# The first partial sum of three of four feature groups formed by two transfers instead of a GpSimd addition, and the third sum moved one up-projection later

## The chip, the cores and the metric

One core of one Trainium2 chip. The metric is the device time of one execution in microseconds (us); smaller is better. Engines: PE is TensorE (PEld its weight load), DVE is VectorE, ACT is ScalarE, POOL is GpSimd, SP is SyncE, which issues transfers only. SPq and POOLq are the queues of instructions that those engines hand out.

## The reference, cut to what matters

Two stages follow each other. The first is a block-wise linear attention with decay: for 4 sequences, 8 heads, 768 positions and head size 64, each block adds a masked product within the block and a product with a running state. The second is a feed-forward pair on the resulting 3072 x 512 rows:

```python
h = x @ w_in                                              # 512 -> 2048
g = np.maximum(h, 0.0) + alpha * np.minimum(h, 0.0)
return (g @ w_out).astype(np.float32)                     # 2048 -> 512
```

## The kernel before

The rows are worked in six chunks c = 0 to 5 of 512 rows each: a chunk is 256 positions of two sequences. For each chunk the attention part leaves its result transposed in `XT[c]`; `up` (L540) then makes one tile of 128 features by four products over the 512 inputs, 128x512 each, and ACT (L553) and DVE (L560) turn it into the f16 tile `g`. Sixteen `up` calls make a chunk's 2048 features. The output product of chunk c runs in the time of chunk c+1, a step of it after each `up` step, so that TensorE alternates between the two. What runs when is written out by hand: the calls stand in program order, each engine's queue keeps that order, and a framework adds the semaphore waits. The order of the last three chunks is in the table `plan` and the loop at L1070 to L1092 (U is one `up`, D one step of the output product).

For chunks 3, 4 and 5 the output product isn't done by 16 plain steps. The product of `g` (split in 2 halves of features and 2 halves of rows) with `w_out` (split in 2 by 2) uses a scheme of Winograd and Strassen with 7 products of half-size blocks instead of 8. `CHAIN` (L640) gives their order: 1, 2, 6, 5, 7, 3, 4. `product` (L642) does eight 128x256 products for one of them and one half b of its rows. Its inputs are sums of blocks of `g`, made by `g_sum` (L627), a 128x512 f16 operation for each of four feature groups j (two feature tiles of each half):

- S1 = a21 + a22, into the tile `s1` (`sums[3]`, one tile for all chunks)
- S3 = a11 - a21, over a21
- S2 = S1 - a11, over a11
- S4 = a12 - S2, over a12

Here a11, a12 are the blocks of the even rows and a21, a22 those of the odd ones. Product 1 reads a11 and product 2 a12 as they are; product 6 reads S2, product 5 reads S1 itself, product 7 reads S3, product 3 reads S4 and product 4 reads a22. S2 overwrites a11, so it comes after product 1; S1 of the next chunk overwrites `s1`, so it comes after product 5 of this one. S3 overwrites a21, so it comes after S1 has read it.

S1 and S3 of group j are made by `sums13` (L721) on POOL, when 10, 12, 14 and 16 `up` calls of the chunk are done (groups 0 to 3); group 3 of the last chunk is made on DVE. S2 and S4 are made on DVE in the next chunk (`sums_at`, L1062), and for the last chunk in `down2_last` (L704): it does products 1 and 2 by halves, then S2 for each half, and ends with products 3 and 4.

SP's queue in this stretch holds the transposing transfers of L311, the last loads, and the stores of the output (L589 for chunks whose output product is plain, L669 and L671 after that); each waits for its own data and is issued in order. POOL's queue holds, besides S1 and S3, `decayed` (L355), `key_decayed` (L291) and the loads of v that it issues (L278).

Of the kernel before, what the change touches and what calls it, by code (L numbers as in the profile page):

```python
# [11 lines left out]
def kernel(  # L12
# [16 lines left out]
    nc = tc.nc  # L29
# [5 lines left out]
    ALU = mybir.AluOpType  # L35
# [124 lines left out]
    for half in range(2):  # L160
# [7 lines left out]
        out=drop, in0=rel_i, scalar1=0.0, scalar2=-1e30, op0=ALU.is_lt, op1=ALU.mult  # L168
# [115 lines left out]
    def engine(x):  # L284
        return nc.gpsimd if x == "G" else nc.vector
# [242 lines left out]
    G = {}  # L528
    O = {}

    def group_of(c, j):
        if (c, j) not in G:
            G[c, j] = g_pool.tile([128, 2, 2, 2, 2, L], fp16, tag=f"g{j}", name=f"g{j}")
        return G[c, j]
# [5 lines left out]
    def up(c, f, bi=None, bank="h"):  # L540
        h_ps = bank_of(bank, "h_ps")
        n = CH if bi is None else W
        for gi in range(NHP):
            x = XT[c][:, gi]
            nc.tensor.matmul(  # L545
                h_ps[:, 0:n] if bi is None else h_ps[:, 0:n].rearrange("p (e j) -> p e j", e=2),
                lhsT=w_in_sb[:, gi, ts(f, 128)],
                rhs=x.rearrange("p e b j -> p (e b j)") if bi is None else x[:, :, bi, :],
                start=(gi == 0),
                stop=(gi == NHP - 1),  # L550
            )
        m = m_pool.tile([128, CH], fp32, tag="m", name="m")
        nc.scalar.activation(m[:, 0:n], h_ps[:, 0:n], AF.Relu, scale=-1.0)  # L553
        g = g_of(c, f)
        if bi is None:
            g, mv, hv = g.rearrange("p e b j -> p (e b j)"), m, h_ps
        else:
            g = g[:, :, bi, :]
            mv, hv = (y[:, 0:n].rearrange("p (e j) -> p e j", e=2) for y in (m, h_ps))
        nc.vector.scalar_tensor_tensor(  # L560
            out=g, in0=mv, scalar=oma[:, f : f + 1], in1=hv, op0=ALU.mult, op1=ALU.add
        )
# [4 lines left out]
    def down(c, t, part, nparts, bank="op"):  # L567
        if part == 0:
            O[c, t] = bank_of(bank, "o_ps")
        o_ps = O[c, t]  # L570
        n = NF // nparts
        for f in range(part * n, part * n + n):
            nc.tensor.matmul(  # L573
                o_ps,
                lhsT=lhs(c, f, t),
                rhs=w_out_sb[:, f, :],
                start=(f == 0),
                stop=(f == NF - 1),
            )
        if part == nparts - 1:  # L580
            store(c, t, o_ps, 0, DM)
            del O[c, t]
# [23 lines left out]
    sums = []  # L606
# [8 lines left out]
    def weight_sum(i, part):  # L615

        p = ds(2 * part, 2)
        (b11, b12), (b21, b22) = [[y[:, p] for y in x] for x in halves]
        w = [sums[x][:, p] for x in range(3)]
        out, in0, in1 = [(w[0], b12, b11), (w[1], b22, w[0]), (w[2], b21, w[1]), (b12, b22, b12)][i]  # L620
        nc.vector.tensor_tensor(out=out, in0=in0, in1=in1, op=ALU.subtract)

    def part_of(c, j, half, e, b=None):
        x = group_of(c, j)[:, half, :, e]
        return x.rearrange("p i b j -> p i (b j)") if b is None else x[:, :, b]

    def g_sum(c, i, j, eng, b=None):  # L627

        a11, a12, a21, a22 = [part_of(c, j, half, e, b) for e in range(2) for half in range(2)]
        s1 = sums[3].rearrange("p f (b j) -> p f b j", b=2)[:, ds(2 * j, 2)]  # L630
        s1 = s1.rearrange("p i b j -> p i (b j)") if b is None else s1[:, :, b]
        out, in0, in1, op = {
            1: (s1, a21, a22, ALU.add),
            3: (a21, a11, a21, ALU.subtract),
            2: (a11, s1, a11, ALU.subtract),
            4: (a12, a12, a11, ALU.subtract),
        }[i]
        engine(eng).tensor_tensor(out=out, in0=in0, in1=in1, op=op)  # L638
# [54 lines left out]
    def down2(c, x):  # L693

        i, side = CHAIN[x // 2]
        b = x % 2
        if b == 0 and i in (1, 2, 5):
            O[c, side] = bank_of("op" if side == 0 else "tk", "o_ps")
        t = O[c, side]
        product(c, i, b, t, b == 0 and i in (1, 2, 5), i in (2, 3, 4) and b == 1, ds(256 * b, 256))  # L700
        if b == 1:
            evacuated(c, i, t)

    def down2_last(c):  # L704
# [3 lines left out]
        for i, side, b in order:  # L708
# [8 lines left out]
            if i == 2 and b == 1:  # L717
                for j in range(4):
                    g_sum(c, 4, j, "V")

    def sums13(c, j, eng="G"):  # L721
        g_sum(c, 1, j, eng)
        g_sum(c, 3, j, eng)
# [346 lines left out]
    for c, at in plan.items():  # L1070
        u = d = w = 0
        for x, what in enumerate(order[c]):
            if x in at:
                at[x]()
            if what == "U":
                up(c, u // 2 + 8 * (u % 2), None, "h")
                u += 1
                if u in (10, 12, 14, 16):
                    sums13(c, u // 2 - 5, "V" if c == 5 and u == 16 else "G")
            elif c == 3:  # L1080
                down(c - 1, d // 4, d % 4, 4, ("op", "tk")[d // 4 % 2])
                d += 1
                for _ in range({1: 1, 3: 1, 4: 1, 7: 1, 8: 1, 10: 1, 11: 2, 12: 1, 14: 1, 15: 2}.get(d, 0)):
                    weight_sum(*divmod(w, 4))
                    w += 1
            else:
                down2(c - 1, d)
                d += 1
            if x in sums_at.get(c, {}):
                g_sum(c - 1, *sums_at[c][x])  # L1090
            if c == 4 and 10 <= x <= 13:
                weight_sum(3, x - 10)  # L1092
# [31 lines left out]
```

## Time and profile before

| what | value |
|---|---|
| runs | median 207.89 us (207.72 to 208.01, 3 runs) |
| profiled execution | 207.7 us, span 205.9 us |
| mean granted TensorE clock | 0.997 |
| DMA over the span | 31.16 MB, mean 151 GB/s |
| DMA in the stretch from 140 to 200 us | 27 to 66 GB/s in steps of 10 us |

The profile records one execution: for each engine its instructions with start, length and, where it stood idle before one, what ended the idle time. A row of the order of time reads: start, length, engine, line, operation, output<-inputs, sizes, and in brackets the idle time and its releaser; several instructions of one kind that follow each other are merged into a row with their count and the whole time they took. Ends of products on TensorE are modelled (they are pipelined), so the distance of their starts is what counts. A row of the view by stretches gives, after the stretch, its length, then busy time and count for PE, PEld, DVE, ACT and POOL, the granted clock, the DMA share and GB/s. A row of the waits gives the total, the number of times and the longest. A row of the transfers gives count, KB each and the median time from issue to landing.

### The profile page before, as it was taken

To read this page: it belongs to the slowest core of one execution; us is meant where nothing else is said; L and a number is where in the kernel's file an instruction comes from. 1 tells how busy PE (TensorE), PEld (TensorE's weight loads), DVE (VectorE), ACT (ScalarE), POOL (GpSimd) and SP (SyncE) were. 2 spreads that over 40 slices of the span, in tenths; PEclk is the share of its full clock that TensorE was granted. 3 is DMA by queue.
4 is the path that set the end of the run, shared out by engine and by line. 5 is a ranking of instruction groups with operands and counts; after the bars stand their busy time and mean duration, and the time that the engine had idled before them with its cause. 6 is when DMAs were issued, how large, how long until landed. Compare 5 with 4: busy or idle time off the path is not lost.

```text
span 205.9 us, 5567 instructions
## 1 busy us (share of the span) xinstructions
PE 200.3 (97%) x2263; PEld 122.8 (60%) x2263; DVE 159.5 (77%) x287; ACT 113.5 (55%) x210; POOL 110.0 (53%) x132
## 2 busy tenths in 40 slices
PE   7999999999999999999999999999999999999993
PEld 6976445556445465555555455467666666666882
DVE  6988889568889847899998897869999467675930
ACT  7896778144777118656766466463453544444321
POOL 8999794043487873295536994193094040553000
PEclk9999999999999999999999999999999999999998
DMA  5999999998999994999879973243001111011222
GB/s 159 280 196 233 244 261 207 233 284 241 224 279 282 198 261 111 232 159 143 170 109 276 212 180 82 42 106 45 30 0 54 51 54 51 2 51 54 75 79 102
DMA packets 58061, 31.16 MB, mean 151 GB/s; under 512 B 27108, under 2 KB 55796, under 8 KB 58036
## 3 DMA queue, kind: packets, MB, share of 16 engines
q1 hardware_dynamic: 42884, 21.25, 41.8%
q0 software_dynamic: 15136, 9.57, 29.2%
q8 instruction: 17, 0.28, 0.5%
q14 instruction: 8, 0.07, 0.1%
q10 hardware_dynamic: 16, 0.00, 0.0%
HBM read 27.27 MB, written 6.29 MB: 163 GB/s over the span
## 4 chain that ended last, share of the span: by engine, by line
PE 89%; ACT 4%; DVE 3%; issue 2%; ACTq 0%; DVEq 0%
PE h_ps L545 39%; PE o_ps L573 21%; PE o_ps L655 16%; PE s L391 3%; PE unread L152 3%; PE acc L416 2%; PE acc L375 2%; PE tpx L341 2%; DVE g L638 1%; PE acc L436 1%; DVE g L560 1%; ACT xT L250 1%; ACT L180 1%; ACT qkT L250 1%; ACT m L553 1%
## 5 line engine op out<-in xcount | busy, mean ns | idle before, releaser
L545 PE MATMUL h_ps<-xT,w_in_sb 128*128 128x512 f16 (+1 forms) x392 | 92.0, 375 | 0.4 <-DVE g L560 0.4
L560 DVE SCALAR_TENSOR_TENSOR g<-m,oma,h_ps 128x512 f16<-128x512 f32 (+1 forms) x98 | 70.9, 733 | 25.4 <-ACT m L553 22.4
L553 ACT ACTIVATE m<-h_ps 128x512 f32<-128x512 f32 (+1 forms) x98 | 57.3, 588 | 47.7 <-PE h_ps L545 40.5
L545 PEld LDWEIGHTS <-w_in_sb 128*128 128x128 f16 x392 | 37.6, 98 | 37.6 <-issue 0.6
L573 PE MATMUL o_ps<-w_out_sb,g 128*128 128x512 f16 x192 | 46.8, 380 | 0.0
L402 DVE TENSOR_TENSOR sm<-s,dmask 128x1024 f16<-128x1024 f32 x24 | 29.2, 1217 | 10.6 <-PE s L391 10.6
L655 PEld LDWEIGHTS <-g 128*128 128x128 f16 x288 | 27.9, 98 | 8.6 <-DVE g L638 0.4
L638 POOL TENSOR_TENSOR s<-g 128x512 f16<-128x512 f16 x11 | 13.0, 1184 | 34.9 <-DVE g L560 18.2
L573 PEld LDWEIGHTS <-g 128*128 128x128 f16 x192 | 17.7, 98 | 19.4 <-DVE g L560 0.2
L250 ACT ACTIVATE xT<-acc 128x512 f16<-128x512 f32 x24 | 14.3, 597 | 24.0 <-PE acc L436 22.2
L355 POOL TENSOR_TENSOR qdT<-qkT,qdecay 128x512 f16<-128x512 f16 (+1 forms) x19 | 20.9, 1102 | 7.3 <-DMA qkT<-qk 4.4
L655 PE MATMUL o_ps<-w_out_sb,g 128*128 128x256 f16 x192 | 24.2, 273 | 0.1
L291 POOL TENSOR_TENSOR kdec<-kraw,kdecay 128x512 f16<-128x512 f32 x18 | 19.1, 1064 | 5.5 <-DMA kraw<-in_k_dram 5.4
L254 POOL CAST qk<-qraw 128x512 f16<-128x512 f32 x12 | 7.4, 620 | 17.7 <-DMA qraw<-in_q_dram 17.7
L465 DVE SCALAR_TENSOR_TENSOR R<-R,rdecay,acc 128x128 f16<-128x128 f16 x54 | 15.4, 337 | 0.0
L278 POOL DMA_DIRECT2D v<-in_v_dram x19 | 14.9, 788 | 0.4 <-issue 0.4
L685 ACT ACTIVATE o_sb<-o_ps 128x512 f32<-128x512 f32 (+1 forms) x16 | 7.8, 490 | 11.3 <-PE o_ps L655 11.3
L638 POOL TENSOR_TENSOR g<-g 128x512 f16<-128x512 f16 x11 | 13.3, 1207 | 0.9
L655 PE MATMUL o_ps<-w_sum,g 128*128 128x256 f16 x96 | 12.3, 273 | 0.0
L391 PE MATMUL s<-qkT 64*64 64x128 f16 x384 | 10.0, 221 | 0.0
L688 DVE TENSOR_TENSOR o_sb<-o_sb,o_ps 128x512 f32<-128x512 f32 (+1 forms) x12 | 6.5, 548 | 4.2 <-PE o_ps L655 2.2
L416 PE MATMUL acc<-sm,v 64*64 64x128 f16 x384 | 9.7, 218 | 0.0
(81 smaller groups left out, 194.0 us busy)
## 6 DMA issues: line engine op xcount, KB each, us to landing
out_dram<-o_sb SPq DMA_DIRECT2D x20, 256.0 KB, 2.7
kraw<-in_k_dram SPq DMA_DIRECT2D x7, 512.0 KB, 5.8
qraw<-in_q_dram SPq DMA_DIRECT2D x6, 512.0 KB, 5.5
v<-in_v_dram POOLq DMA_DIRECT2D x19, 128.0 KB, 5.8
w_in_sb<-in_moe_w_in_dram POOLq DMA_DIRECT2D x4, 512.0 KB, 8.5
w_out_sb<-in_moe_w_out_dram POOLq DMA_DIRECT2D x4, 512.0 KB, 10.6
qraw<-in_q_dram POOLq DMA_DIRECT2D x6, 256.0 KB, 7.2
qraw<-in_q_dram SPq DMA_DIRECT2D x6, 256.0 KB, 4.6
```

The lines of the kernel that those rows point to most:

```text
L250: nc.scalar.activation(out, in_, AF.Copy)
L291: engine(eng).tensor_tensor(out=kdec, in0=kr, in1=kdecay[:, ds(4 * hh, 4), :].rearrange("p h e -> p e h").unsqueeze(3).to_broadcast([128, ...
L355: engine(eng).tensor_tensor(out=qdT[:, :, :, p], in0=(t["qps"] if eng == "P" else t["qkT"][:, 0])[:, :, :, p], in1=qdecay[:, hh, :, :, p], ...
L391: nc.tensor.matmul(t["s"][ds(a * 64, 64), hl, hp, 1 - e, :].rearrange("p (e j) -> p e j", e=2), lhsT=t["qkT"][p, 1, e, hp, ds(a * 64, 64)] ...
L402: nc.vector.tensor_tensor(out=t["sm"].rearrange("p a h x j -> p (a h) x j"), in0=t["s"].rearrange("p a h x j -> p (a h) x j"), in1=mask_of ...
L465: nc.vector.scalar_tensor_tensor(out=R[b, hh, m + 1][:, hp], in0=R[b, hh, m][:, hp], scalar=rdecay[:, 2 * hh + hp : 2 * hh + hp + 1], in1= ...
L545: nc.tensor.matmul(h_ps[:, 0:n] if bi is None else h_ps[:, 0:n].rearrange("p (e j) -> p e j", e=2), lhsT=w_in_sb[:, gi, ts(f, 128)], rhs=x ...
L553: nc.scalar.activation(m[:, 0:n], h_ps[:, 0:n], AF.Relu, scale=-1.0)
L560: nc.vector.scalar_tensor_tensor(out=g, in0=mv, scalar=oma[:, f : f + 1], in1=hv, op0=ALU.mult, op1=ALU.add)
L573: nc.tensor.matmul(o_ps, lhsT=lhs(c, f, t), rhs=w_out_sb[:, f, :], start=(f == 0), stop=(f == NF - 1),)
L638: engine(eng).tensor_tensor(out=out, in0=in0, in1=in1, op=op)
L655: nc.tensor.matmul(t[:, cols], lhsT=x, rhs=w, start=(fresh and f == 0), stop=(last and f == NF // 2 - 1), skip_group_check=True,)
```

## The change

For groups 0, 1 and 2 of each of the chunks 3, 4 and 5, S1 is made by two transfers instead of POOL's addition: SP issues a copy of a21 into `s1` when 10, 12 or 14 `up` calls are done, and one `up` later POOL makes S3 (as before) and then issues a transfer of a22 that adds to `s1`. Group 3 is as before. The added functions stand behind `down2_last`, so lines after L719 move down: the copy is line 728 and the adding transfer line 732 of the new kernel.

```diff
+    def s1_of(c, j):
+
+        a21, a22 = [part_of(c, j, half, 1) for half in range(2)]
+        return sums[3][:, ds(2 * j, 2)], a21, a22
+
+    def s1_begun(c, j):
+        s1, a21, a22 = s1_of(c, j)
+        nc.sync.dma_start(out=s1, in_=a21)
+
+    def s1_added(c, j):
+        s1, a21, a22 = s1_of(c, j)
+        nc.gpsimd.dma_start(out=s1, in_=a22, accum_op=ALU.add)
...
                 up(c, u // 2 + 8 * (u % 2), None, "h")
                 u += 1
-                if u in (10, 12, 14, 16):
-                    sums13(c, u // 2 - 5, "V" if c == 5 and u == 16 else "G")
+                if u in (10, 12, 14):
+                    s1_begun(c, u // 2 - 5)
+                if u in (11, 13, 15):
+                    g_sum(c, 3, u // 2 - 5, "G")
+                    s1_added(c, u // 2 - 5)
+                if u == 16:
+                    sums13(c, 3, "V" if c == 5 else "G")
```

In the queues this gives: POOL's nine S1 additions of groups 0 to 2 are gone and nine adding transfers, each behind its S3, are added; each S3 waits for its copy to land. In chunk 3 `decayed` of L355, that stood between S3 of group 0 and S1 of group 1, stands ahead of S3 of group 0, and the next one ahead of S3 of group 2. On SP the copies of chunk 3 stand ahead of the transpose of L311 at 120.13 us, behind it, and ahead of the transpose at 127.19 us (behind the store at 126.11 us). In chunks 4 and 5 the copies alternate with the stores of the previous chunk's output tiles: store of the tile that product 2 ends, copy of group 0, store (product 7), copy of group 1, store (product 3), copy of group 2, store (product 4). The copy of group j in chunks 4 and 5 also waits for product 5 of the chunk before and for the adding transfer of the same group there.

## The prediction

> **What bounds the kernel now.** I read the totals first, then the stretches of the second half, the waits of TensorE, and the order of time around its gaps.
>
> ```profile
> span 205.9 us, 5567 instructions
> PE 200.3 (97%) x2263; PEld 122.8 (60%) x2263; DVE 159.5 (77%) x287; ACT 113.5 (55%) x210; POOL 110.0 (53%) x132
> ...
> 140.00:150.00 10.00, 9.61 (x141) 6.75 (x140) 9.58 (x20) 4.36 (x9) 2.05 (x2) 1.00 0.08 28
> 150.00:160.00 10.00, 9.87 (x103) 6.33 (x102) 9.13 (x15) 4.14 (x8) 6.59 (x6) 1.00 0.08 28
> ...
> PEld L655 <- DVE g L638: 0.4, 1, 0.4
> PE h_ps L545 <- DVE g L560: 0.4, 1, 0.4
> ...
> 142.92 1.03 PE L545 MATMUL h_ps<-xT,w_in_sb 128*128 128x512 f16 x4
> 143.78 1.04 PE L655 MATMUL o_ps<-w_sum,g 128*128 128x256 f16 x8
> 145.22 1.02 PE L545 MATMUL h_ps<-xT,w_in_sb 128*128 128x512 f16 x4 [0.40 <-DVE g L560]
> ...
> 155.95 1.35 PE L655 MATMUL o_ps<-w_out_sb,g 128*128 128x256 f16 x8
> 157.14 1.03 PE L545 MATMUL h_ps<-xT,w_in_sb 128*128 128x512 f16 x4
> ```
>
> TensorE sets the time. A step of four wide or eight narrow products starts 0.87 us after the one before (142.92 and 143.78), and nearly all the region that the change touches (from about 115 us on) goes at this pace. Two places fall short, both where DVE is over 90% busy: 143.78 to 145.22 is 1.44 us, 0.57 too long, and 155.95 to 157.14 is 1.19 us, 0.32 too long. So 0.89 us is about all that lighter engines could win. POOL, from which the change takes work, is no bound; it matters through DVE, whose f16 sums stretch beside POOL's:
>
> ```profile
> L638 DVE TENSOR_TENSOR g<-g x13: 414/417/1305, 150.5 to 195.6; 128x512 f16<-128x512 f16 x13
> L638 POOL TENSOR_TENSOR s<-g x11: 1147/1152/1338, 115.5 to 184.7; 128x512 f16<-128x512 f16 x11
> ...
> 137.16 1.06 POOL L291 TENSOR_TENSOR kdec<-kraw,kdecay 128x512 f16<-128x512 f32 x1
> 137.31 2.32 DVE L638 TENSOR_TENSOR g<-s,g 128x512 f16<-128x512 f16 x1
> 138.17 1.16 POOL L355 TENSOR_TENSOR qdT<-qkT,qdecay 128x512 f16<-128x512 f16 x1
> ...
> 149.30 1.15 POOL L638 TENSOR_TENSOR s<-g 128x512 f16<-128x512 f16 x1 [7.32 <-PE o_ps L655]
> 151.94 1.15 POOL L638 TENSOR_TENSOR s<-g 128x512 f16<-128x512 f16 x1
> 152.07 1.30 DVE L638 TENSOR_TENSOR g<-g 128x512 f16<-128x512 f16 x1
> ```
>
> The first DVE sum took 2.32 us, until just after the two POOL operations beside it (139.33), and the second 1.30 instead of 0.42.
>
> **The change, part by part.** *POOL.* Nine S1 sums go, 9 x 1.15 = 10.4 us. Nine issues of an adding transfer come. No row shows one; the nearest is the issue of the 128 KB load, 0.79 us, so 7.1 us come back. POOL has idle stretches here (7.32 us ahead of 149.30), so the difference of 3.3 us is worth nothing by itself. Through DVE it is: in chunk 4 S3 of group 0 must now wait for its copy (issued when the products of line 655 that read S1 let go, 149.3 us, where POOL's S1 stands now; landed about 151.5), and S1 of group 1 no longer stands beside the DVE sum of 152.07. That sum meets only the end of S3 (152.7) and ends about 0.3 us earlier, and the last g sum before 157.14 with it: I take **-0.3 us**, with 0 and -0.89 as ends. The wait of 145.22 stays: its cause at 137.31 is the key decay of line 291 and line 355, which the change leaves where they are, since S1 and S3 of group 3 stay on POOL ahead of them.
>
> *SP.* Nine copies are queued in program order, and each also stands behind what precedes it. In chunk 3 they stand ahead of two transposes (line 311) that POOL needs only microseconds later; they wait for tiles long finished, so each costs its issue, about 0.37 us by the store rows below. In chunks 4 and 5 they alternate with the stores of the chunk before, and a store waits for its evacuation. So the copy of group 2 can't start before that of chunk 4's third output tile is stored, however early its data are ready. This is the part that costs.
>
> ```profile
> 184.71 1.15 POOL L638 TENSOR_TENSOR s<-g 128x512 f16<-128x512 f16 x1 [2.46 <-DVE g L560]
> 185.94 1.16 POOL L638 TENSOR_TENSOR g<-g 128x512 f16<-128x512 f16 x1
> 186.22 0.68 DVE L688 TENSOR_TENSOR o_sb<-o_sb,o_ps 128x512 f32<-128x512 f32 x1
> 186.92 0.37 SPq L669 DMA_DIRECT2D out_dram<-o_sb  x1
> 183.45 3.84 SPq L669 DMA_DIRECT2D out_dram<-o_sb  x2
> ...
> out_dram<-o_sb SPq DMA_DIRECT2D x20, 256.0 KB, 2.7
> out_dram<-o_sb SPq DMA_DIRECT2D x8, 128.0 KB, 1.9
> v<-in_v_dram POOLq DMA_DIRECT2D x1, 128.0 KB, 4.1
> ...
> L278 POOL DMA_DIRECT2D v<-in_v_dram x19: 752/791/901, 5.1 to 136.3; - x19
> DMA to landing us min/median/max: 3.3/5.8/11.5
> ...
> 189.93 3.66 PE L655 MATMUL o_ps<-w_out_sb,g 128*128 128x256 f16 x32
> 192.35 1.70 DVE L638 TENSOR_TENSOR g<-s,g 128x256 f16<-128x256 f16 x8
> 193.43 1.91 PE L655 MATMUL o_ps<-w_sum,g 128*128 128x256 f16 x16
> 195.17 1.91 PE L655 MATMUL o_ps<-w_sum,s 128*128 128x256 f16 x16
> 196.92 2.78 PE L655 MATMUL o_ps<-w_out_sb,g 128*128 128x256 f16 x24
> ...
> 193.97 0.74 DVE L688 TENSOR_TENSOR o_sb<-o_sb,o_ps 128x256 f32<-128x256 f32 x2
> 194.63 1.42 DVE L638 TENSOR_TENSOR g<-g 128x512 f16<-128x512 f16 x4
> ```
>
> *The last chunk, group 2, step by step.* The store waits for the sum that ends at 186.90 and is issued at 186.92; the copy follows at 186.92 + 0.37 = 187.29. A copy within SBUF has no row: the 128 KB stores land in 1.9 us and the 256 KB ones in 2.7 at the median; behind a store just issued I take 2.2, so 189.5. S3 must wait for it, since it overwrites the source of the copy (until now POOL began group 2's S1 at 184.71 and was through with its S3 at 187.1): 1.16 us and a little for the semaphore, 190.7. The adding transfer goes out then. Its landing is the unknown. Bounds from the rows: 1.9 us (a plain transfer of 128 KB) and 5.8 (the median of POOL's 128 KB loads, most of them beside other traffic). It is nearest to POOL's own loads with little beside them, 3.3 at the least and 4.1 for the last one; it reads two streams, so I take 4.1: landed at **194.8**.
>
> *Who needs it.* The eight DVE sums of 192.35 (1.70/8 = 0.21 us apart; four groups for half 0, then four for half 1) read S1 group by group; group 2's first stands at 192.78. Behind it in DVE's order wait the other sums, the two evacuations of 193.97 and the four sums of 194.63. TensorE reads what it writes in the 5th of the 16 products of 193.43, which are 0.109 us apart (16 until 195.17): at 193.86. The shorter f16 sum takes 0.28, so it may begin up to 193.58, and the first sum of half 1, two places later, gives the same limit (194.30 - 0.28 - 2 x 0.21 = 193.60); with a little for the semaphore, 193.55. Landing at 194.8 is late by **1.25 us**. From there nothing gives it back: the products of 195.17 and of 196.92 follow in order at full pace. Nothing is added either: the four sums of 194.63 would end at 196.05 + 1.25 = 197.3, and what reads them, the last 8 of the 24 products of 196.92, starts at 198.66 + 1.25. Group 1 is in time: its copy follows the store of 183.45, so its add goes out near 187.3 and, by 4.1, has landed by 191.4; group 0 is earlier.
>
> *Chunks 3 and 4* go by the same chain, with room:
>
> ```profile
> 126.11 0.36 SPq L589 DMA_DIRECT2D out_dram<-o_sb  x1
> L669 SPq DMA_DIRECT2D out_dram<-o_sb x1: 372/372/372, 160.2 to 160.2; - x1
> 165.61 1.15 POOL L638 TENSOR_TENSOR s<-g 128x512 f16<-128x512 f16 x1 [6.51 <-DVE g L560]
> 169.72 0.75 DVE L638 TENSOR_TENSOR g<-s,g 128x512 f16<-128x512 f16 x2
> ```
>
> The store of 160.2 lets the last copy of chunk 4 out at 160.6; landed 162.8, S3 until 164.0, add landed at 168.1 by 4.1 and 169.8 by 5.8. The sum that reads it is the second of 169.72, about 170.05. Group 3's POOL sum at 165.61 stays in place, as the add's issue ends at 164.8. In chunk 3 the last copy follows the store of 126.11; copy, S3 and add by the same times end near 134, and nothing is wanted before 137.31.
>
> *Sum.* +1.25 - 0.3 = +0.95 us on the profiled execution's 207.7 us (span 205.9 and 1.8 around it): **208.7 us**. That execution is 0.2 below the median of the runs shown, 207.89, well within what they scatter; I keep 208.7. Its own range: adds that land 3.3 to 5.8 us after their issue, the copy 1.9 to 2.7, and a DVE gain of 0 to 0.3 give 0.15 to 3.45 us late, 207.6 to 211.2.
>
> The page "DMA: Bandwidth & Descriptors" of the Trainium skill (section "Anatomy of one DMA — SWDGE (gpsimd) path") gives about 2.0 us plus bytes/436,000 for a transfer issued by GpSimd, which makes an estimate of 2.3 us for 128 KB. By that the add lands at 193.0, before the limit, and the sum would be -0.3 us. The trace's own loads from that queue are all slower (3.3 at the least), though they come from HBM.
>
> **The rivals.**
> 1. *The add lands early and is hidden* (this side is not slower). The mechanism is the 193.55 limit: with the copy at 1.9 and the add at up to 3.1 us, nothing is late, and only the DVE gain is left: 207.7 - 0.3 = 207.4. For it: the queues are nearly empty then, and source and target are both in SBUF. Against: no transfer of POOL's queue landed under 3.3 us. It decides at a landing of about 2.9 us after issue by my 190.7. The rule of "DMA: Bandwidth & Descriptors" above is this case.
> 2. *POOL's relief shifts both DVE jams*, and TensorE's two waits close, with the add hidden as in 1: 207.7 - 0.89 = 206.8. Against it: what stands beside the sum of 137.31 isn't moved.
> 3. *The add is slow*, as an addition at the target that reads before it writes could be. Half way between the rows' median and maximum, 8.65 us: the last chunk is late by 190.7 + 8.65 - 193.55 = 5.8, and chunk 4's sum waits until 172.65 instead of 170.05, of which perhaps 2 us reach TensorE: 207.7 + 5.8 + 2 - 0.3 = 215.2.
> 4. *The change doesn't relieve POOL at all*, because issuing an addition keeps POOL as long as the sum did (1.15 instead of 0.79), and the copies get out early enough otherwise: 207.7, no change.
>
> **How the numbers follow.** Forecast 0.62; rival 1 0.18, rival 2 0.08, rival 3 0.08, rival 4 0.04. About 0.2% (0.42 us) is what a measurement of this kernel can tell from no change. Slower: 0.58 of the forecast's 0.62 and rival 3, 0.66. Same: the forecast's 0.04, 0.11 of rival 1 and rival 4, 0.19. Faster: the rest of rival 1 and rival 2, 0.15. The range takes in rival 1 and the forecast's own range: 207.3 to 211.2. It leaves out rivals 2 and 3.
>
> **What would show it.** In the changed profile: SP issues the last copy right after the store near 186.9; POOL's S3 of group 2 ends near 190.7; DVE waits for a DMA of S1 at its third half sum; TensorE stops inside the 16 products after 193.4 for about 1.25 us and runs at 0.87 a step elsewhere; the sum of 152.07 falls below 1.1 us. It is wrong if the add lands within 3 us of its issue, if TensorE also stops near 170 us, or if the copies go out ahead of the stores.

## The result and the profile after

| | before | changed |
|---|---|---|
| median of 5 runs each | 207.86 us (207.72 to 208.01) | 210.62 us (210.53 to 211.92) |
| ratio | | 1.016 (95% interval 1.0141 to 1.0178) |
| profiled execution, span | 207.7 us, 205.9 us | 211.92 us, 209.7 us |

The profiled execution of the changed kernel is the slowest of its five; the spans of the other four are 208.3 to 208.7 us. Its totals, from the page:

```profile
span 209.7 us, 5597 instructions
PE 201.3 (96%) x2263; PEld 122.9 (59%) x2263; DVE 164.3 (78%) x287; ACT 113.6 (54%) x210; POOL 109.3 (52%) x132
```

POOL's busy time hardly fell (110.0 to 109.3; the rows of the nine issues are 1.2 us long, but reach into what follows them), and DVE, whose work is unchanged, is busy 4.8 us longer. The stretches of the changed kernel say where TensorE stands still, and its waits say for whom:

```profile
120.00:130.00 10.00, 9.57 (x122) 5.04 (x112) 9.74 (x11) 5.58 (x11) 7.38 (x8) 1.00 0.79 163
130.00:140.00 10.00, 7.99 (x45) 4.29 (x44) 7.95 (x13) 4.60 (x8) 5.27 (x6) 1.00 0.66 61
...
POOL g L638 <- DMA s<-g: 38.1, 6, 10.7
PE h_ps L545 <- DVE g L560: 2.9, 4, 1.6
```

The same two stretches of the kernel before:

```profile
120.00:130.00 10.00, 10.00 (x98) 4.98 (x91) 8.30 (x15) 5.76 (x11) 6.84 (x7) 1.00 0.51 103
130.00:140.00 10.00, 10.00 (x63) 6.00 (x62) 7.29 (x11) 5.73 (x10) 5.23 (x5) 1.00 0.35 66
```

Between 120 and 140 us TensorE was never idle before; now it misses 2.44 us there, in chunk 3, where the forecast had put no cost. The same instructions of both traces, by their starts: TensorE is 0.40 us behind at the step of line 573 that began at 114.77 before the change and begins at 115.17 now; 3.21 behind at the `up` step of 133.22 (136.43 now); 3.20 at the start of the tail (189.93 and 193.13); 3.89 at the products that read S1 (195.17 and 199.06). So 0.40 us is lost before the first of the new transfers (119.05 us), where the order of the work is the same in both. It is there already at the first `up` product (17.59 us before, 18.02 now), and the profiled executions of all the kernels below begin that product between 17.26 and 18.03 us, so it isn't put down to the change. From there on it is **2.8 us in chunk 3, nothing in chunks 4 and 5, and 0.69 in the tail**.

In order of time, chunk 3 of the changed kernel:

```profile
119.05 0.72 SPq L728 DMA_DIRECT2D s<-g  x1
...
122.62 1.15 POOL L638 TENSOR_TENSOR g<-g 128x512 f16<-128x512 f16 x1 [5.43 <-DMA s<-g]
122.87 1.18 DVE L621 TENSOR_TENSOR w_sum<-w_out_sb,w_sum 128x512 f16<-128x512 f16 x1
123.71 1.23 POOL L732 DMA_DIRECT2D s<-g  x1
...
124.51 1.22 POOL L278 DMA_DIRECT2D v<-in_v_dram  x1
124.63 3.58 DVE L621 TENSOR_TENSOR w_sum<-w_out_sb,w_sum 128x512 f16<-128x512 f16 x2
...
125.30 1.50 POOL L291 TENSOR_TENSOR kdec<-kraw,kdecay 128x512 f16<-128x512 f32 x1
...
126.32 1.60 POOL L638 TENSOR_TENSOR g<-g 128x512 f16<-128x512 f16 x1
...
128.22 2.07 POOL L355 TENSOR_TENSOR qdT<-qkT,qdecay 128x512 f16<-128x512 f16 x1
...
128.79 2.90 DVE L621 TENSOR_TENSOR w_sum<-w_out_sb,w_sum 128x512 f16<-128x512 f16 x1
128.92 1.02 PE L545 MATMUL h_ps<-xT,w_in_sb 128*128 128x512 f16 x4 [0.43 <-DVE g L560]
...
129.95 1.45 POOL L638 TENSOR_TENSOR g<-g 128x512 f16<-128x512 f16 x1
...
132.40 1.02 PE L545 MATMUL h_ps<-xT,w_in_sb 128*128 128x512 f16 x4 [1.59 <-DVE g L560]
```

The first copy is issued at 119.05, behind the store of line 589 at 118.58. POOL stands 5.43 us, until that copy has landed, and then works off all that piled up behind S3 in one train, from 122.6 to about 132.6 us (the lengths of its rows overlap; starts count). DVE's weight sums of line 621, two f16 inputs each and 0.42 us alone, fall into it. Of the two of 124.63 the first took 0.61 us while POOL only issued transfers, the second 3.05:

```profile
L621 DVE TENSOR_TENSOR w_sum<-w_out_sb,w_sum x2: 607/1826/3045, 124.6 to 125.2; 128x512 f16<-128x512 f16 x2
```

It started at 125.2 and ended at 128.2, after the key decay and S3, which followed each other without a gap. The next one stood 2.90 us for line 355 and the last S3. In the kernel before, these three sums began in a gap in POOL's work:

```profile
124.27 0.75 DVE L621 TENSOR_TENSOR w_sum<-w_out_sb,w_sum 128x512 f16<-128x512 f16 x2
...
125.92 0.42 DVE L621 TENSOR_TENSOR w_sum<-w_out_sb,w_sum 128x512 f16<-128x512 f16 x1
...
126.08 1.27 POOL L638 TENSOR_TENSOR s<-g 128x512 f16<-128x512 f16 x1 [2.68 <-DVE g L560]
```

Behind the sums in DVE's queue is line 560, which empties the banks that `up` fills: TensorE stops, for 0.43 us at 128.92, for 1.59 at 132.40, and for 0.42 at 134.71, while DVE is still behind.

The tail of the changed kernel, in order of time, with the landing of the adds and of the copies (least, median, most, of the eight of nine adds and the five of nine copies whose landing the trace holds):

```profile
190.13 0.37 SPq L669 DMA_DIRECT2D out_dram<-o_sb  x1
...
190.60 0.61 SPq L728 DMA_DIRECT2D s<-g  x1
...
192.99 1.14 POOL L638 TENSOR_TENSOR g<-g 128x512 f16<-128x512 f16 x1 [1.24 <-DVE g L560]
...
194.09 1.18 POOL L732 DMA_DIRECT2D s<-g  x1
...
196.63 0.60 PE L655 MATMUL o_ps<-w_sum,g 128*128 128x256 f16 x4
197.37 1.30 DVE L638 TENSOR_TENSOR g<-s,g 128x256 f16<-128x256 f16 x6 [1.33 <-DMA s<-g]
197.72 1.48 PE L655 MATMUL o_ps<-w_sum,g 128*128 128x256 f16 x12 [0.49 <-DVE g L638]
...
DMA to landing us min/median/max: 3.1/3.4/5.5
...
DMA to landing us min/median/max: 2.2/2.5/3.4
```

This is the forecast's chain: store, copy, S3, add, a DVE sum that waits for the transfer, TensorE stopping at the 5th of 16 products. The row of S3 names line 560, of which an operation ended at 192.98, as what ended the wait. But that is the 15th `up` call's, and S3 of group 2 reads tiles of the first twelve; the copy landed at 192.82.

Not in the span at all is a further part: the five runs of the changed kernel have 2.2 us outside it, those of the kernel before 1.8.

### The profile page after: what moved, and what is told of

It is laid out like the page before. It is cut to its first block, busy times and chain, and to the rows that moved or that the text cites. A ratio compares the mean times of both kernels' runs of the same rounds, so it can differ in the third digit from the quotient of the medians.

```text
span 209.7 us, 5597 instructions
## 1 busy us (share of the span) xinstructions
PE 201.3 (96%) x2263; PEld 122.9 (59%) x2263; DVE 164.3 (78%) x287; ACT 113.6 (54%) x210; POOL 109.3 (52%) x132
## 4 chain that ended last, share of the span: by engine, by line
PE 81%; DVE 10%; ACT 3%; issue 2%; DMA 2%; POOL 1%; ACTq 0%; DVEq 0%
PE h_ps L545 35%; PE o_ps L573 18%; PE o_ps L655 13%; DVE w_sum L621 3%; PE s L391 3%; DVE g L560 3%; PE unread L152 3%; PE acc L416 3%; PE acc L375 2%; PE tpx L341 2%; DVE g L638 2%; DMA s<-g 2%; ACT m L553 1%; DVE sm L402 1%; PE acc L436 1%
## 5 line engine op out<-in xcount | busy, mean ns | idle before, releaser
L355 POOL TENSOR_TENSOR qdT<-qkT,qdecay 128x512 f16<-128x512 f16 (+1 forms) x19 | 22.0, 1165 | 6.8 <-DMA qkT<-qk 5.0
L278 POOL DMA_DIRECT2D v<-in_v_dram x19 | 15.4, 818 | 0.3 <-issue 0.3
L732 POOL DMA_DIRECT2D s<-g x9 | 11.6, 1287 | 0.0
L254 POOL CAST qk<-kraw 128x512 f16<-128x512 f32 x9 | 5.5, 614 | 7.9 <-DMA kraw<-in_k_dram 7.9
```

The costliest lines, as they stand in the source:

```text
L278: nc.gpsimd.dma_start(out=v16.rearrange("p h e d -> p h (e d)"), in_=v[2 * (c % 2) + bi, ds(4 * hh, 4), ds((c // 2) * W, W), :].rearrange( ...
L355: engine(eng).tensor_tensor(out=qdT[:, :, :, p], in0=(t["qps"] if eng == "P" else t["qkT"][:, 0])[:, :, :, p], in1=qdecay[:, hh, :, :, p], ...
```

## The experiments

Theory A: in chunk 3 the wait of S3 for its copy makes a train on POOL, DVE's f16 sums stand beside it, and TensorE waits for DVE; the tail's late add is a second, smaller cost. Theory B: the forecast's chain is the whole loss. Rival C: issuing the adding transfers, or their traffic, is what costs in chunk 3. Each kernel was timed against the kernel before on the same chip: 207.76 us for the first four kernels below; 207.53 for the second timing of the weight sums moved earlier and for the two kernels of the last experiment; 207.71 for the others.

**The change in chunk 3 alone**

```diff
+                if c != 3 and u in (10, 12, 14):
+                    sums13(c, u // 2 - 5, "G")
-                if u in (10, 12, 14):
+                if c == 3 and u in (10, 12, 14):
                     s1_begun(c, u // 2 - 5)
-                if u in (11, 13, 15):
+                if c == 3 and u in (11, 13, 15):
```

> The two transfers stand only in chunk 3; chunks 4 and 5 make S1 on POOL as before. Theory A (pile-up): in chunk 3 POOL waits 5.4 us for the first copy, then runs its operations in one train, and the weight sums of line 621 on DVE stand until gaps in that train; TensorE loses some 2.1 to 2.8 us there. A expects 207.86 + 2.1 to 2.8 = 210.0 to 210.7. Theory B (the forecast's chain: the whole loss is the last add landing late): chunk 3 costs nothing, 207.9.

Measured: 209.58 us, ratio 1.0096 (1.0079 to 1.0112). B is out: two thirds of the loss are made in chunk 3, where no S1 lands late. TensorE waits for DVE at the same three steps (0.97, 0.49 and 0.42 us, in an execution of 209.96 us). The size, 1.8, is under A's figure, which came from the profiled execution of 211.92 us; why the stop is longer in some executions is not shown.

**The change in chunks 4 and 5 alone** (the same edit with `c == 3` and `c != 3` exchanged)

> The two transfers stand only in chunks 4 and 5; chunk 3 makes S1 on POOL as before. A: only the tail's stop is left, 0.65 us in the changed kernel's trace (196.63 to 197.72 instead of 0.44), so 207.86 + 0.65 = 208.5. B: the whole loss, 210.6.

Measured: 208.43 us, ratio 1.0035 (1.0022 to 1.0047), 0.67 us: A's figure. The two parts add to 2.5 of the 2.8; of the rest, 0.2 is the part outside the span, which has grown by 0.4 us with all the transfers, by 0.2 in chunk 3 alone and not at all here.

**Weight sums moved later**

```diff
-{1: 1, 3: 1, 4: 1, 7: 1, 8: 1, 10: 1, 11: 2, 12: 1, 14: 1, 15: 2}
+{1: 1, 3: 1, 4: 1, 7: 1, 8: 1, 10: 1, 13: 1, 14: 2, 15: 2, 16: 1}
```

> The changed kernel, with the three weight sums of line 621 that stand behind the 11th and 12th down steps of chunk 3 moved to behind the 13th, 14th and 16th; all else alike. A says that these f16 sums of DVE are what POOL's train stops: without them in its stretch the stop of chunk 3 falls from 2.8 us to under 0.8, and the time to 208.5 to 209.4. If instead the train costs TensorE in another way (a contended memory, the transfers themselves), nothing moves: 210.6.

Measured: 210.36 us, ratio 1.0132 (1.0098 to 1.0166): outside what A expected. Its trace, in order of time, shows why it doesn't decide: one moved sum stood in the train again, and a stop of TensorE of over 1 us was left in chunk 3. Another 1.0 us is lost near 145 us, where POOL's key decay and line 355, later than before, held a DVE sum of line 638 for 2.61 us (2.32 before) and TensorE stops twice (0.41 and 0.77 us; before, once for 0.40).

```profile
128.01 2.09 POOL L355 TENSOR_TENSOR qdT<-qkT,qdecay 128x512 f16<-128x512 f16 x1
...
128.28 2.11 DVE L621 TENSOR_TENSOR w_sum<-w_out_sb,w_sum 128x512 f16<-128x512 f16 x1
...
132.75 1.02 PE L545 MATMUL h_ps<-xT,w_in_sb 128*128 128x512 f16 x4 [1.13 <-DVE g L560]
```

**Copies of chunk 3 earlier**

```diff
-                if u in (10, 12, 14):
-                    s1_begun(c, u // 2 - 5)
+                for j in range(3):
+                    if u == ((6, 9, 13)[j] if c == 3 else 10 + 2 * j):
+                        s1_begun(c, j)
```

> The changed kernel, with the copies of chunk 3 issued when 6, 9 and 13 up calls are done instead of 10, 12 and 14; S3 and the adds stay where they are. A: POOL no longer waits 5.4 us for the first copy, so its operations are spread again; the stop of chunk 3 shrinks to under 1 us, 208.5 to 209.6. If the adding transfers' issues on POOL, or their traffic, are what costs, they are all still there: 210.6.

Measured: 208.76 us, ratio 1.0061 (1.0038 to 1.0084); nine of ten executions between 208.47 and 209.03, one at 211.03, of which there is no trace. POOL begins its first S3 without a wait (at 116.90 us, where it was 116.71 before the change) and waits 2.36 and 4.12 us ahead of the other two, so that its operations are spread. All adds, copies and S3 are still there, and 1.8 of the 2.8 us are gone; the trace has no stop of TensorE between 100 and 140 us. What costs in chunk 3 is when POOL works, not what it issues; C is out for that part.

**Weight sums moved earlier**

```diff
+{1: 1, 3: 1, 4: 1, 7: 2, 8: 2, 9: 2, 14: 1, 15: 2}
```

> The changed kernel, with the four weight sums of chunk 3 that stand behind down steps 10 to 12 moved to behind steps 7, 8 and 9, ahead of POOL's train (which lasts from about 122.5 to 132.5 us). The first try moved them later, and one of them fell into the train's end. Theory A: with no two-input f16 sum of DVE beside the train, TensorE loses less than 0.4 us in chunk 3, and only the tail's stop is left: 208.2 to 208.9. If the train or the transfers cost TensorE in another way: 210.4 to 210.8.

> The same kernel as weight_sums_earlier, whose six executions fell in two groups (208.3 twice, 209.5 to 209.8 four times), while the profiled one was of the first and showed no stop of TensorE in chunk 3. Another profile, to see what the second group has: if a stop in chunk 3 beside POOL's train again, a sum of DVE stands in the train in some executions and not in others; if a stop elsewhere, the moved sums cost there. About 4 chances in 6 of catching it.

Measured: 209.61 us, ratio 1.0075 (1.005 to 1.01), outside both bands, with two executions at 208.3 and four at 209.5 to 209.8; the second time 208.70 us, ratio 1.0053 (1.0038 to 1.0067), inside A's band, all at 208.66 to 209.06. Both profiles (208.3 and 209.06 us) show POOL's wait of over 5 us, the train behind it and no stop of TensorE beside it. The second one, in order of time:

```profile
122.78 1.15 POOL L638 TENSOR_TENSOR g<-g 128x512 f16<-128x512 f16 x1 [5.48 <-DMA s<-g]
...
128.39 2.08 POOL L355 TENSOR_TENSOR qdT<-qkT,qdecay 128x512 f16<-128x512 f16 x1
128.40 1.04 PE L545 MATMUL h_ps<-xT,w_in_sb 128*128 128x512 f16 x4
129.28 1.03 PE L573 MATMUL o_ps<-w_out_sb,g 128*128 128x512 f16 x4
130.14 1.03 PE L545 MATMUL h_ps<-xT,w_in_sb 128*128 128x512 f16 x4
```

POOL still waits 5.48 us and TensorE keeps its 0.87 us a step: in these two executions, without a sum of line 621 in its first 8 us, the train costs nothing. No profile was caught of the four executions near 209.7; what they have stays open.

**A copy, then POOL's own sum**

```diff
+                if c == 3 and u in (10, 12, 14):
+                    s1_begun(c, u // 2 - 5)
+                if c == 3 and u in (11, 13, 15):
+                    sums13(c, u // 2 - 5, "G")
+                if c != 3 and u in (10, 12, 14):
+                    sums13(c, u // 2 - 5, "G")
```

> Chunk 3 alone, and no adding transfer: the copies go out as in the changed kernel, but POOL then makes S1 by its own sum over the copy (so the copy has no use) and S3, one up call later. Chunks 4 and 5 as before. Theory A (the wait for the copy makes the train, whatever the train holds): the loss stays as in the kernel with chunk 3 alone (209.58 against 207.76) or grows, 209.3 to 210.6. Rival C (issuing the additions on POOL, or their traffic, is what costs): it vanishes, 207.6 to 208.1.

Measured: 209.46 us, ratio 1.0091 (1.0075 to 1.0107), as much as the change in chunk 3 alone, without one adding transfer. C is out here too: the wait for a copy costs this much with no add at all, and every stop of TensorE is again a wait for DVE. But that the two totals agree is chance, for only part of the loss lies in the same place. By the starts of the `up` steps 0.6 us is lost in chunk 3, and 1.1 us near 145 us, behind a DVE sum of line 638 that stood 2.80 us for the key decay and line 355 (2.32 before). In order of time:

```profile
122.50 1.15 POOL L638 TENSOR_TENSOR s<-g 128x512 f16<-128x512 f16 x1 [5.37 <-DMA s<-g]
...
124.51 3.65 DVE L621 TENSOR_TENSOR w_sum<-w_out_sb,w_sum 128x512 f16<-128x512 f16 x2
...
128.87 1.02 PE L545 MATMUL h_ps<-xT,w_in_sb 128*128 128x512 f16 x4 [0.47 <-DVE g L560]
...
144.43 0.39 PE L655 MATMUL o_ps<-w_sum,g 128*128 128x256 f16 x2 [0.59 <-DVE g L638]
...
147.33 1.02 PE L545 MATMUL h_ps<-xT,w_in_sb 128*128 128x512 f16 x4 [0.77 <-DVE g L560]
```

**All copies earlier** (in chunks 4 and 5 when 10, 10 and 12 `up` calls are done, in chunk 3 as above)

> The changed kernel, with the copies issued earlier in all three chunks: when 6, 9 and 13 up calls are done in chunk 3, when 10, 10 and 12 are done in chunks 4 and 5, so that the copies of groups 1 and 2 stand one store earlier in SP's queue. If the forecast's chain of the last chunk holds (store, copy, S3, add), group 2's add lands over 3 us earlier and the tail's stop of 0.6 us goes: 207.5 to 208.1. If the tail's stop has another cause, it stays, as in the kernel with early copies in chunk 3 alone: 208.76.

Measured: 208.26 us, ratio 1.0026 (1.0016 to 1.0036), a little over the expected band. The tail's stop shrank from 0.69 to 0.17 us (1.91 instead of 1.74 from 193.50 to 195.41 in its trace) but did not go: group 2's copy, issued at 184.01, ran beside the add of group 1 and a 256 KB store (issued at 183.53), and copy and add were slow. Its transfers between 183.5 and 190 us, with KB and us to landing:

```profile
s<-g POOLq DMA_DIRECT2D x1, 128.0 KB, 6.2
s<-g SPq DMA_DIRECT2D x1, 128.0 KB, 5.0
```

Its span, 206.0 in the median, is that of the kernel before (205.9); what is left of the loss lies outside the span (2.24 us, against 1.80).

**Group 2 of chunk 5 by POOL's sums** (the change in chunks 4 and 5 alone, with `sums13` for that one group)

> Chunks 4 and 5 changed, chunk 3 as before, and group 2 of chunk 5 made by POOL's sums as before. The forecast's chain: the one late landing is group 2 of chunk 5, so 207.6 to 208.0. If the other transfers of chunks 4 and 5 cost something too, it stays near the 208.43 of the kernel with chunks 4 and 5 alone.

Measured: 207.50 us, ratio 0.9986 (0.9977 to 0.9996), a little under the expected band. The one late landing is the whole loss of chunks 4 and 5. In the profiled execution it is under the kernel before by a lead that it has before its first transfer (148.89 us), most of it at the first `up` product already (17.30 us against 17.59), so that no part of it is shown to be the change's. TensorE's step of line 655 in this kernel and in the kernel before:

```profile
135.46 1.04 PE L655 MATMUL o_ps<-w_out_sb,g 128*128 128x256 f16 x8
```

```profile
135.81 1.04 PE L655 MATMUL o_ps<-w_out_sb,g 128*128 128x256 f16 x8
```

**The old stop near 144 us**: the preparation of the last unit moved ahead of S1 of group 3, in the kernel before and in the last one

```diff
+            29: lambda: prepared(23),
         },
         4: {
-            2: lambda: prepared(23),
```

> The kernel before, with one call moved: the preparation of the last attention unit (two casts on ACT, the load of v and the key decay of line 291 on POOL) stands three up steps earlier, in POOL's idle time ahead of S1 of group 3. No transfer for S1. Tests the reading that two-input f16 sums of DVE stand until a gap in POOL's row of operations: the DVE sum that took 2.32 us beside the key decay and line 355 back to back then meets at most the end of one operation. If that is so, the sum falls below 1.2 us, TensorE's stop of 0.57 us near 144 us goes, and the time to 207.71 - 0.4 to 0.6 = 207.1 to 207.3. If DVE is late there for another reason, 207.7.

> The kernel with the transfers in chunks 4 and 5 but not for group 2 of chunk 5 (207.50 measured), with the same call moved. The two gains should add: 206.9 to 207.1, under both kernels. If the gain of either was only a shift, 207.3 to 207.6.

Measured: 207.52 us, ratio 0.9996 (0.9981 to 1.001), and 207.27 us, ratio 0.9982 (0.9972 to 0.9993). The first is a miss: no gain in time, though the sum fell from 2.32 to 0.49 us. In order of time, another sum then met line 355, and TensorE's stop only shrank (142.54 and two steps of 0.87 make 144.28; it starts 0.37 us later, where it was 0.57):

```profile
136.93 0.49 DVE L638 TENSOR_TENSOR g<-s,g 128x512 f16<-128x512 f16 x1
...
140.40 1.29 DVE L638 TENSOR_TENSOR g<-s,g 128x512 f16<-128x512 f16 x1
...
142.54 1.03 PE L545 MATMUL h_ps<-xT,w_in_sb 128*128 128x512 f16 x4
...
144.65 1.02 PE L545 MATMUL h_ps<-xT,w_in_sb 128*128 128x512 f16 x4 [0.21 <-DVE g L560]
```

The second is the fastest kernel of the study, 0.2% under the kernel before; it lies between the two bands expected, at the edge of the second, and how much of it is each edit's, these runs don't separate.

## Why the prediction was right and wrong, point by point

**What bounds the kernel**: held. TensorE's pace is 0.87 us a step wherever nothing stops it, in every trace.

**POOL** ("the difference of 3.3 us is worth nothing by itself") and **chunk 3** ("so each costs its issue", "with room"): this step failed, and it is two thirds of the loss. The forecast checked when S1 was wanted in chunk 3 and found microseconds to spare; that was right, nothing waited for S1 there. It did not follow the other side of the new wait: the first S3 stood for its copy (itself behind the store of 118.58 on SP, and 0.61 to 0.72 us to issue, not 0.37), POOL's order behind it was delayed into one train, and DVE's sums of line 621, three of which before began in POOL's idle time, stood beside it. The rows for it were shown (2.32 us until two POOL operations were over), and were used only for the 0.3 us gain. The runs: 1.8 us for chunk 3 alone, a loss of that size without any add (part of it later, near 145 us), no stop once the copies came earlier, none in the two profiles with the sums out of the train. That 210.62 lies within the forecast's range is luck: the upper part of the range was meant for an add that lands 5.8 us after its issue, and the one that mattered landed after 3.2. The page "SBUF — State Buffer" of the Trainium skill (section "Who interferes with whom") says that a DVE operation with two SBUF inputs contends with a GpSimd operation that reads SBUF, and that the one that issues first blocks the other fully until it is over. The trace agrees that it is a full block on one side (POOL's starts are 1.02 and 1.10 us apart beside the standing sum, no more than the lengths of these operations alone), but it was DVE that stood, though its row begins 0.14 us before the key decay's, and for two POOL operations in a row (3.05 us), not for one.

**The last chunk's chain**: right in every step, with one term too large, the landing of the add. Store to copy, copy to S3, S3 to add went as forecast (with TensorE 3.2 us behind, the copy was due at 190.5 and came at 190.60; the add was due at 193.9 and came at 194.09). The landing was 3.2 us instead of 4.1. With the 0.2 us by which the add went out later and 0.1 from its landing to the DVE sum, 1.25 comes down to about 0.6; the stop was 0.69 us. Taking that chain away for the one group gave back the whole 0.67 us of chunks 4 and 5.

**The gain of 0.3 us on DVE**: didn't come. The sum of 152.07 (155.30 now) fell from 1.30 to 0.93 us, as forecast, but the steps whose starts were 155.95 and 157.14 are as far apart as before. The sum on which TensorE waits there began at 156.44 and begins at 159.64, exactly the 3.20 us later that everything is: ahead of it stands line 560, which in both traces waits for ACT (DVE is idle for 0.10 and 0.06 us before it). The sum that ended 0.3 us earlier in front of that wait didn't bring it forward; the forecast had linked the two without looking at what stands between them:

```profile
155.30 0.93 DVE L638 TENSOR_TENSOR g<-g 128x512 f16<-128x512 f16 x1
...
159.15 1.35 PE L655 MATMUL o_ps<-w_out_sb,g 128*128 128x256 f16 x8
...
159.64 0.42 DVE L638 TENSOR_TENSOR g<-g 128x512 f16<-128x512 f16 x1
...
160.34 1.03 PE L545 MATMUL h_ps<-xT,w_in_sb 128*128 128x512 f16 x4
```

**Chunk 4**: held, nothing was late, and the wait of 145.22 stayed (0.41 us at 148.45). **The issue of an add** keeps POOL 0.80 us (123.71 to 124.51), as taken from the loads, though its row is 1.2 long.

**The rivals**: an early landing (rival 1) asked for 2.9 us or less; the least was 3.1. By the rule of the page "DMA: Bandwidth & Descriptors" of the Trainium skill (section "Anatomy of one DMA — SWDGE (gpsimd) path"; an estimate of 2.3 us) nothing would have been late; the trace is against it from issue to landing, 3.1 to 5.5. The slow add (rival 3, 8.65) and no relief of POOL (rival 4) did not come either. None of the rivals had a wait on POOL that moves its work under DVE's.

**Not forecast**: about 0.4 us outside the span. Kernels with all nine copies and adds have 2.2 us there, the kernel before 1.8, those with the change in chunk 3 alone 2.0, in chunks 4 and 5 alone 1.75, and the last of these with group 2 of chunk 5 by POOL's sums 2.0 again. It follows neither the number of transfers nor that of waits; its cause was not found.

## What to carry to other kernels

When a step gains a wait, ask not only who needs its result but where its engine's later work will fall, and which other engine's operations will then stand beside it. An engine that is off the path can be delayed for free only if the place to which it is delayed is free too. A transfer that another engine must wait for should be issued as soon as its source is ready, ahead of stores that wait for something else in the same queue.

## What the runs showed of the hardware that was not expected

- A two-input f16 sum of DVE (0.42 us alone) stood 3.05 us for two POOL operations that followed each other, and ran in 0.61 us while POOL only issued transfers.
- A copy of 128 KB within SBUF landed in 2.2 us alone and in 5.0 beside an adding transfer of 128 KB and a 256 KB store; that adding transfer took 6.2 us, where those with little beside them took 3.1 to 3.4.
